# Three constant tables loaded in part and completed on the chip, mirrored x columns, a new order list (2-D spectral filter with a gate, one Trainium2 core)

## The chip, the cores and the metric

One core of a Trainium2 chip. Its engines are TensorE (PE; the loading of its stationary operand is shown apart as PEld), VectorE (DVE), ScalarE (ACT), GpSimd (POOL) and SyncE (SP), which here only issues DMAs. Each engine runs its own queue of instructions in order and waits at semaphores for the others. The metric is the device time of one execution in microseconds, the median of several runs.

## The reference

x has 2048 rows (S) and 1024 columns (D), in bf16. The sigmoid of each row's product with a gate vector gives g. x is taken through a real 2-D FFT, multiplied by two complex weight arrays (A and B), each product goes back through the inverse FFT, and the two results are mixed row by row:

```python
g = sigmoid((x * gate_w).sum(-1, keepdims=True))
X = rfft2(x)
a = irfft2(X * (A_w_r + 1j * A_w_i))
b = irfft2(X * (B_w_r + 1j * B_w_i))
return g * a + (1 - g) * b
```

## The kernel before

All transforms are matmuls with constant tables. A row index is s1 + 16 * s2, so the length-2048 transform is done in two factors, 128 and 16, with a twiddle between them; columns are split into four quarters of 256, folded by symmetry into an even half (par 0, units 0 to 7) and an odd half (par 1, units 8 to 15). The stages:

1. `F1` (f1, L336): for each s1 and each parity (e, o) 8 matmuls of 128x128 over s2, into PSUM. The fold y = a + b, a - b (L422) is done for 24 of the 32 pieces on DVE (`FC`, a copy of one half to SBUF by ACT, then `FD`, two additions on DVE) and for 8 on POOL, which can't read PSUM (`FX`, a copy of the whole by ACT or DVE, then `FP`, two additions on POOL). The copies go to eight slots of the tile wx.
2. For each of 16 units n: `F2` (L528, the column transform with the table FD, two tiles tt), `T` (its copy, by ACT or DVE: all copies stand on L201 for ACT, L203 for DVE), `F3` (L569, the twiddle and 16-point transform with the tables WF and WN; WN is the negated second half of WF, made by `neg`, L280), `X` (its copy), `P` (L586, the product with the weights W, one DVE instruction of 4096 elements), `J` (L632, the inverse 16-point transform with the table WJ) and two copies `R` into rl, which `H` (L654) stores to a scratch in DRAM. For units 0 to 7 the column 0 needs the partner row: `Y` (PE, table PM), `NA` (L609, DVE, with the pair weights WP) and `N` (L615, DVE), which patches the product before `J` reads it.
3. The gate: `gc` (L285 to L297, thirteen small instructions on POOL) makes its stationary operand gwz, `GH` (L447) multiplies it with y on PE, then `GC`, `Gt`, `GK`, `GZ`, `GS` (sigmoid on ACT), `GA` and `GB` (L515, L519, DVE) make the gate-weighted tables EA and EB from E.
4. `pw` (L313 to L320, eight small instructions on POOL) makes WP from w0.
5. `L` (L665) loads the scratch back, turned: eight loads of 512 KB for par 0 into re, eight for par 1 into ro. `V` (L675, with EA and EB), its copy `VC`, then the last transform with the table IG: `C` (i3f, L712) and `U` (i3, L703). For the even half `EX`, `EQ`, `E`, `ES`, `EF` (copies and the sum and difference, L796 and L806) write EV; for the odd half `OR` (L826, DVE), or `OC` and `OP` (ACT, then POOL, L822), or `QD` and `QP` (DVE, then POOL, L833 and L838) add and subtract, and `S` (L847) stores.

The order of everything is the list ORDER, written out by hand: each token is a call, for example `FD:3:e`, `P:1:b`, or `R:15:0:D`, whose last letter is the engine (A, D, P; S for the SP queue, on which all loads `x`, `c`, `W`, `L` and stores `H`, `S` stand). Each engine gets its instructions in the order of the list, whatever the others do. PSUM banks are the digits at the end of PE's tokens.

The tables WF, WJ and IG hold each value several times: WF is block-sparse (half of each block zero), WJ has six blocks of which three are others negated or exchanged, IG has its second half negated as a third block. All are loaded whole from DRAM. The lines that hold them:

```python
c["F1"] = _bf16np(np.concatenate([F, -F, F], axis=1))
G = np.concatenate([IG[:, 0], IG[:, 1], -IG[:, 1]], axis=-1)
c["IG"] = _bf16np(G.transpose(2, 0, 1, 3))
lh = C["WJ"][r, 2 * u + tt, w:w + 64]
```

Of the kernel before, what the change touches and what calls it, by code (L numbers as in the profile page):

```python
# [39 lines left out]
P:5:b NA:5:D N:5:D F3:6:6 J:4:2:0 F2:8:0:5 P:7:b X:6:A Y:6:4 NA:6:D R:4:0:A P:6:b R:4:1:A T:8:0:A J:5:2:6 F2:9:0:1 R:5:0:A  # L40
Y:7:0 F2:9:1:5 R:5:1:A F3:8:2 NA:7:D T:9:0:D F2:10:1:0 T:9:1:D F2:10:0:4 X:8:A T:10:1:A N:7:D GA:D:8 T:10:0:A F3:9:2 GA:D:4
W:S:14 H:2:1 X:9:A J:7:6:0 N:6:D GA:D:0 P:8:b J:6:2:4 W:S:12 H:2:0 R:7:1:A H:3:1 R:6:0:D W:S:15 R:7:0:A H:5:0 H:5:1 GB:D:4
P:9:b H:4:1 R:6:1:A F3:10:0 H:4:0 X:10:A H:7:1 F2:11:0:6 F2:11:1:7 F2:12:0:4 H:6:0 F2:12:1:5 F2:13:1:0 F2:14:1:1 P:10:b
T:11:0:A T:11:1:A T:12:0:A T:12:1:A F3:11:6 J:8:4:2 X:11:A F3:12:6 T:14:1:A R:8:0:A T:13:1:A F2:13:0:1 GB:D:0 R:8:1:D
# [867 lines left out]
```

## Time and profile before

| | us |
|---|---|
| median of 3 runs | 114.50 (114.27 to 114.72) |
| the profiled execution | 114.51 |
| its span, first to last instruction | 112.7 |
| DVE busy | 100.1 (89%) |
| PE busy | 99.4 (88%) |
| ACT busy | 86.2 (76%) |
| POOL busy | 43.0 (38%) |
| DMA: 36.79 MB | 326 GB/s over the span |

A row of the timeline gives the start, the length, the engine, the line, the operation, the output and input with their shapes, and how many instructions were merged; in brackets the idle time before it and what ended that. Instructions on one engine overlap a little at their ends, so the step from one start to the next is less than the length shown. In the chain of waits a row is the start, the time, and what the end of the kernel waited for.

### The profile page before, as it was taken

Reading aid. Unit: us, or ns where it says so; the run is one execution under the profiler, and the core shown is the slowest. Engines: PE = TensorE matmul, PEld = TensorE weight load, DVE = VectorE, ACT = ScalarE, POOL = GpSimd, SP = SyncE. Lnnn points to the kernel's source line nnn. Section 1 sums busy time; section 2 is a strip of 40 time slices with the busy share of each in tenths; the row PEclk is TensorE's granted clock in tenths of the full one; section 3 lists DMA queues with packets and bytes.
Section 4 is the critical chain, followed back from the end, with each engine's and each line's share of the span. In section 5 each row is a group of like instructions: output and inputs, shape, how many; then the busy total and the mean of one; then the engine's idle time right before and its main releaser. Section 6 shows DMA issues by size and latency. Waiting matters only on the chain.

```text
span 112.7 us, 3824 instructions
## 1 busy us (share of the span) xinstructions
PE 99.4 (88%) x1556; PEld 69.8 (62%) x1559; DVE 100.1 (89%) x160; ACT 86.2 (76%) x141; POOL 43.0 (38%) x64
## 2 busy tenths in 40 slices
...
DVE  0278999999999999999999999999999678999770
ACT  4176887899999999999999999998867934435300
POOL 3187969700000000000000007178702269999760
...
DMA  3999999989999999985799999999889998444994
GB/s 70 368 309 398 405 379 400 398 260 413 410 412 412 372 298 326 394 298 186 237 302 292 420 407 307 385 377 325 295 246 398 337 385 329 196 192 186 372 372 186
DMA packets 17794, 36.79 MB, mean 326 GB/s; under 512 B 1904, under 2 KB 10736, under 8 KB 17776
## 3 DMA queue, kind: packets, MB, share of 16 engines
...
q10 hardware_dynamic: 288, 0.10, 0.4%
...
## 4 chain that ended last, share of the span: by engine, by line
PE 32%; DVE 27%; DMA 16%; ACT 10%; issue 7%; SPq 4%; DVEq 1%; ACTq 0%
DVE p L586 9%; DVE y L422 9%; PE ps L703 8%; DMA ro<-sc 6%; DMA re<-in_x_dram 5%; DVE rl L203 5%; PE ps L632 5%; PE ps L528 5%; PE ps L675 5%; DMA sc<-rl 5%; ACT rl L201 4%; PE ps L569 4%; ACT T L201 3%; SPq L665 3%; PE ps L336 3%
## 5 line engine op out<-in xcount | busy, mean ns | idle before, releaser
L806 POOL TENSOR_TENSOR re<-wx 128x256 f32<-128x256 f32 x10 | 10.7, 1089 | 55.8 <-ACT wx L201 55.8
L201 ACT COPY wx<-ps 128x256 f32<-128x256 f32 (+1 forms) x41 | 18.3, 475 | 8.0 <-PE ps L336 4.5
L201 ACT CAST rl<-ps 128x1024 bf16<-128x1024 f32 x23 | 22.8, 1069 | 0.8 <-PE ps L632 0.6
L201 ACT CAST V<-ps 128x512 bf16<-128x512 f32 x26 | 14.9, 616 | 8.8 <-PE ps L675 4.4
L632 PE MATMUL ps<-p,wj 32*64 32x512 bf16 x512 | 18.2, 380 | 1.1 <-ACT rl L201 0.6
L528 PE MATMUL ps<-fd,y 128*128 128x256 bf16 x128 | 17.1, 273 | 1.3 <-ACT T L201 0.8
L586 DVE TENSOR_TENSOR p<-X,ro 128x4096 bf16<-128x4096 bf16 x8 | 18.2, 2278 | 0.0
L201 ACT CAST X<-ps 128x1024 bf16<-128x1024 f32 x16 | 17.3, 1079 | 0.1
L422 DVE TENSOR_TENSOR y<-ps,wx 128x256 bf16<-128x256 f32 x48 | 16.4, 414 | 0.5 <-ACT wx L201 0.5
L336 PE MATMUL ps<-f,re 128*128 128x128 bf16 x256 | 15.2, 219 | 1.6 <-DMA re<-in_x_dram 1.5
L336 PEld LDWEIGHTS <-re 128*128 128x128 bf16 x256 | 14.6, 98 | 2.4 <-DMA re<-in_x_dram 2.2
L201 ACT CAST T<-ps 128x512 bf16<-128x512 f32 x26 | 15.5, 647 | 0.5 <-PE ps L528 0.3
L528 PEld LDWEIGHTS <-y 128*128 128x128 bf16 x128 | 11.3, 97 | 5.9 <-issue 4.5
L632 PEld LDWEIGHTS <-wj 32*64 32x64 bf16 x512 | 8.3, 103 | 7.6 <-issue 4.1
L422 POOL TENSOR_TENSOR y<-wx 128x256 bf16<-128x256 f32 x16 | 11.3, 732 | 2.6 <-ACT wx L201 2.1
L826 DVE TENSOR_TENSOR ot<-re,ps 128x512 bf16<-128x512 f32 x18 | 11.3, 682 | 0.9 <-PE ps L703 0.4
L703 PE MATMUL ps<-ig,V 128*128 128x512 bf16 x45 | 11.2, 379 | 0.2
L712 PE MATMUL ps<-ig,V 128*128 128x256 bf16 x80 | 10.9, 273 | 0.2 <-ACT rl L201 0.2
L203 DVE CAST rl<-ps 128x1024 bf16<-128x1024 f32 x9 | 10.9, 1215 | 0.2 <-PE ps L632 0.2
L569 PE MATMUL ps<-T,wf 64*64 64x512 bf16 (+1 forms) x128 | 10.1, 333 | 1.1 <-DVE rl L203 0.4
L838 POOL TENSOR_TENSOR ot<-pq 128x512 bf16<-128x512 f32 x8 | 10.0, 1281 | 0.0
L675 PEld LDWEIGHTS <-re 128*128 128x128 bf16 x128 | 7.8, 98 | 2.4 <-issue 1.3
...
## 6 DMA issues: line engine op xcount, KB each, us to landing
...
```

Source lines behind the costliest of these rows:

```text
L201: nc.scalar.copy(out=out, in_=in_)
L203: Q[e].tensor_copy(out=out, in_=in_)
L336: nc.tensor.matmul(o, lhsT=lh, rhs=rh, start=(h == 0), stop=(h == 1))
L422: Q[e].tensor_tensor(yo[:, v, k:k + n, s1, :], a.rearrange("p (k c) -> p k c", c=4), b.rearrange("p (k c) -> p k c", c=4), op)
L528: nc.tensor.matmul(ps[:, v * 256:v * 256 + 256], lhsT=y[:, v, par, b, 2 * t:2 * t + 2, :, :].rearrange("p j s c -> p (j s c)"), rhs=C["FD" ...
L569: nc.tensor.matmul(view(ps[ho, tt * 512:(tt + 1) * 512], dst), lhsT=lh, rhs=view(T[hp(jh), tt, :], src), start=(w == 0), stop=(w == 1))
L586: nc.vector.tensor_tensor(p[:], xb, wb, ALU.mult)
L632: nc.tensor.matmul(o, lhsT=lh, rhs=src[r, ri, wi, tt], start=(q == 0), stop=(q == 3))
L675: nc.tensor.matmul(ps[:, ch * 128:ch * 128 + 128], lhsT=RR[par][:, v, ch // 2, s, c0 + 256 * ab:c0 + 256 * ab + 128], rhs=Ew[:, s1, :], st ...
L703: nc.tensor.matmul(ps, lhsT=Vs[par, v][:, s, ch, :], rhs=rh, start=(ch == 0), stop=(ch == 3))
L712: nc.tensor.matmul(ps[:, o:o + 256], lhsT=Vs[par, v][:, s, ch, :], rhs=g[:, o:o + 256], start=(ch % 2 == 0), stop=(ch % 2 == 1))
L826: nc.vector.tensor_tensor(otile(v)[:, s, h, :], EV[:, v, s], PS["O", 1, v, s], (ALU.add, ALU.subtract)[h])
```

## The change

- **Tables.** F1 keeps two of three blocks. WF is loaded with 32 instead of 64 columns a block into a part of the tile EA that is free until `GS`, and `kW` (spread_wf) writes both halves of each block by two scales with a mask per partition. WJ is loaded with its first 64 of 192 columns, and `kJ` makes the other two blocks: 0 negates the whole, 1 negates every second pair, 2 copies the other pairs. IG is loaded with 1024 of 3072 columns, and `kI` (spread_ig, six parts) makes the mirrored and negated blocks with a sign per partition. `mk` (signs) makes masks and signs from a column of F1.
- **Mirrored columns.** Each quarter of x has its second 128 columns in reverse, on the host's side and in the tables FD and IG, so that the second half of an IG block is the first times a sign.
- **Where.** On POOL: `kW:0:4:1`, `kJ:0:4` 0, 1 and 2, `kW:4:16` 0 and 1, `kJ:4:16:2`, and all six `kI`; on DVE: `mk`, `kW:0:4:0`, `kJ:4:16` 0 and 1. `gc` and `pw` come after `kJ:4:16:2` on POOL.
- **Order.** A new list. Between engines move: one `FX`, net two `R`, one `T`, three `VC`, `E` from DVE to ACT; two `X`, one each of `EX`, `OC`, `ES` from ACT to DVE; two `EQ` from DVE to POOL. Loads: W:3, PM and both parts of WJ earlier; FD:1:2, W:2, EZ and IG later or among others; W:13 earlier; `H:8` before the `L:0`, `L:0:3` with the other `L:0`; the sequence of `L:1` is 1, 3, 6, 0, 5, 7, 2, 4 instead of 1, 3, 6, 7, 0, 2, 4, 5.
- `prod_part`, the argument `at` of load_w and the changed i3_half are called by neither list.

```diff
 ORDER = """
-warm:8 c:A:F1 x:S:0:1 x:S:1:1 c:A:gws F1:0:o:4 x:S:2:2 F1:0:e:1 F1:1:e:6 F1:1:o:5 FC:0:e:A FC:1:e:A tab:A x:S:4:2 x:S:6:2
-c:S:E x:S:8:2 FX:0:o:D x:S:10:2 FD:0:e FD:1:e F1:2:e:7 F1:3:e:2 F1:3:o:0 FX:1:o:D FC:3:e:A F1:2:o:5 F1:5:e:4 x:S:12:2
-c:S:WF:0:4 x:S:14:2 c:S:w0 gc:P FP:0:o FX:3:o:A FP:1:o FC:2:e:D F1:4:e:6 FC:5:e:A FD:2:e FD:3:e c:S:FD:0:1 c:S:WJ:0:4
...
-FP:7:o FP:5:o pw:P F1:12:o:4 FC:14:e:A F1:8:o:1 F1:10:o:5 FC:12:o:A FC:8:o:A FD:14:e FC:10:o:A neg:D:0:4 neg:D:4:16 FD:13:o
-F2:1:1:2 F2:1:0:6 F2:0:0:3 FC:15:o:A T:1:1:A FD:10:o FD:8:o FD:12:o T:1:0:A W:S:2 W:S:6 T:0:0:A F1:14:o:7 F2:0:1:5 F1:11:o:6
-T:0:1:A F3:1:2 FD:15:o FC:11:o:A F2:2:0:5 F2:2:1:4 FC:14:o:A X:1:A F3:0:0 FD:11:o T:2:0:A T:2:1:A X:0:A F2:4:1:6 F2:3:1:5
-FD:14:o Y:1:4 T:3:1:A P:1:b F2:4:0:3 F2:3:0:2 Y:0:7 F3:2:0 GH:5 T:3:0:A T:4:0:A NA:1:D W:S:10 W:S:5 P:0:b W:S:3 W:S:7
-c:S:WJ:4:16 F3:3:3 X:2:A W:S:9 NA:0:D T:4:1:A W:S:11 N:1:D W:S:4 GC:A J:1:6:0 F2:5:0:2 F2:5:1:5 P:2:b X:3:A R:1:1:A R:1:0:A
...
-V:0:2:0:2 VC:0:2:1:A VC:0:2:0:A EX:1:1:A H:12:0 J:14:0:4 J:13:6:2 R:14:0:A P:15:b H:11:1 R:14:1:A R:13:0:A C:0:2:1:1
-C:0:2:0:5 EX:2:0:A H:12:1 EX:2:1:D V:0:1:0:4 GB:D:12 R:13:1:D J:15:0:6 V:0:6:1:5 VC:0:1:0:A C:0:1:0:2 R:15:1:A V:0:6:0:4
-H:14:0 H:14:1 GB:D:8 R:15:0:D H:13:0 H:13:1 VC:0:6:1:A H:15:1 H:15:0 VC:0:6:0:A V:0:4:1:3 V:0:5:1:6 L:0:3 EX:1:0:A L:1:1
-L:1:3 L:1:6 EQ:0:0:1:D C:0:6:1:0 V:0:5:0:4 VC:0:5:1:D VC:0:5:0:D E:6:1:A EQ:2:1:0:D EQ:0:1:1:P L:1:7 L:1:0 L:1:2 L:1:4
...
-OR:7:1:0 S:S:7:0 OR:7:1:1 S:S:6 OP:4:0:0 OP:4:0:1 OR:4:1:1 OR:4:1:0 S:S:7:1 S:S:4
+warm:8 c:A:F1 x:S:0:1 x:S:1:1 c:A:gws x:S:2:2 mk:D F1:0:o:1 F1:0:e:4 c:S:WF:0:4 x:S:4:2 x:S:6:2 x:S:8:2 c:S:PM c:S:WJ:0:4
+F1:1:o:5 x:S:10:2 c:S:E x:S:12:2 F1:1:e:0 x:S:14:2 tab:A FX:0:o:A W:S:3 c:S:w0 F1:2:o:7 FC:0:e:D FC:1:e:A F1:2:e:1 FP:0:o
+c:S:FD:0:1 c:S:WF:4:16 W:S:0 FD:0:e c:S:WJ:4:16 W:S:1 FX:1:o:A kW:0:4:1:P FD:1:e kW:0:4:0:D FX:2:o:D FC:2:e:A FP:1:o F1:3:e:4
+FP:2:o F1:3:o:0 FC:3:e:A neg:D:0:4 FD:2:e FD:3:e FX:3:o:A FP:3:o F1:5:e:3 F1:4:e:6 F1:5:o:5 FC:5:e:A FC:4:e:A FD:5:e FD:4:e
+F1:6:e:0 F1:7:e:1 kJ:0:4:1:P kJ:0:4:0:P F1:7:o:2 kJ:0:4:2:P F1:8:e:7 F1:9:e:4 FC:6:e:A FD:6:e F1:9:o:6 FC:7:e:A FX:7:o:A
...
+F1:14:e:1 F1:10:o:5 FC:15:e:A FC:12:o:A FC:14:e:A FP:4:o F1:13:o:3 F1:14:o:4 FC:10:o:A FD:13:e FC:13:o:A FC:14:o:A F1:8:o:6
+FD:15:e FC:8:o:A FD:14:e F2:1:0:1 F2:0:0:7 FD:10:o FD:13:o F1:15:o:0 kW:4:16:1:P FD:14:o T:1:0:A F2:1:1:5 F2:0:1:3 T:0:0:A
+F1:11:o:1 FD:8:o FC:15:o:A T:1:1:A T:0:1:A F3:1:6 c:S:FD:1:2 FD:12:o W:S:2 kW:4:16:0:P W:S:10 W:S:7 W:S:6 FD:15:o F3:0:3
+FC:11:o:A FD:11:o X:1:A X:0:A F2:2:0:2 W:S:4 W:S:5 W:S:9 W:S:11 F2:4:1:0 F2:2:1:5 F2:3:1:6 kJ:4:16:2:P gc:P Y:1:7 neg:D:4:16
+P:1:b pw:P T:2:1:A c:S:IG T:2:0:A F2:3:0:1 F2:4:0:4 F3:2:2 GH:5 T:3:1:A T:3:0:A X:2:A Y:0:6 T:4:0:A T:4:1:A F3:3:2 P:0:b
+NA:1:D NA:0:D N:1:D J:1:6:0 P:2:b F2:7:1:4 GC:A X:3:A R:1:0:A R:1:1:A Gt:2 Y:2:3 F2:5:0:5 T:5:0:A c:S:EZ N:0:D NA:2:D
+F2:5:1:3 H:1:0 W:S:8 H:1:1 T:5:1:A F3:4:6 P:3:b Y:3:5 T:7:1:A NA:3:D kJ:4:16:1:D F2:7:0:3 J:0:0:4 N:3:D X:4:A T:7:0:A kI:0:P
+kJ:4:16:0:D kI:3:P GK:D J:3:2:6 R:0:0:A kI:1:P R:0:1:D R:3:1:A Y:4:5 GZ:0:0 F2:6:1:4 F3:5:6 GS:0 N:2:D R:3:0:D H:0:0 NA:4:D
...
+H:10:1 EQ:1:0:1:P R:13:1:A H:10:0 H:12:1 GB:D:8 V:0:7:0:6 VC:0:7:0:A H:12:0 V:0:2:0:4 C:0:2:1:5 EQ:0:1:0:P VC:0:2:0:A
+EQ:1:1:0:P J:15:0:2 H:11:1 EX:2:1:A H:14:0 R:15:0:A R:15:1:D C:0:2:0:6 V:0:7:1:5 H:13:0 H:13:1 H:14:1 VC:0:7:1:A V:0:3:1:7
+V:0:5:0:4 C:0:7:0:2 C:0:7:1:1 EQ:1:1:1:D VC:0:5:0:A EX:7:0:A H:15:0 EQ:0:1:1:P H:15:1 V:0:5:1:0 V:0:3:0:4 V:0:4:0:2 EX:2:0:D
+EQ:2:1:1:D EQ:2:0:1:D VC:0:3:0:D VC:0:5:1:A kI:5:P EQ:1:0:0:P EQ:0:0:0:P EQ:7:0:1:P C:0:5:0:5 VC:0:3:1:A kI:4:P EQ:7:0:0:P
+EX:7:1:A L:1:1 L:1:3 C:0:5:1:3 L:1:6 L:1:0 VC:0:4:0:A C:0:3:1:4 V:0:6:1:7 C:0:3:0:0 V:0:4:1:1 V:0:6:0:6 L:1:5 L:1:7
+EQ:0:0:1:P EQ:7:1:1:P EQ:2:1:0:P EQ:7:1:0:P E:3:1:A ES:5:1:A ES:5:0:D EQ:2:0:0:D L:1:2 EF:5:0 C:0:4:0:2 EF:5:1 VC:0:6:1:A
...
     return 8 * t + 4 * (i % 2) + i // 2
+
+
+NF = 3 if "FG:" in ORDER else 2
+
+
+def quarter_order():
+    return np.concatenate([np.arange(128), 255 - np.arange(128)])
 def make_constants():
...
     F = F.reshape(128, 128)
-    c["F1"] = _bf16np(np.concatenate([F, -F, F], axis=1))
+    c["F1"] = _bf16np(np.concatenate([F, -F, F][:NF], axis=1))
     c["E"] = _bf16np(E)
...
     c["ID"] = _bf16np(np.eye(128))
-    j = np.arange(256) - 255.5
+    j = quarter_order() - 255.5
     i = np.arange(256)
...
     IG = IG.reshape(2, 2, 2, 128, 256)
-    G = np.concatenate([IG[:, 0], IG[:, 1], -IG[:, 1]], axis=-1)
-    c["IG"] = _bf16np(G.transpose(2, 0, 1, 3))
+    G = np.concatenate([IG[0, 0, :, :, :128], IG[0, 1, :, :, :128]], axis=-1)
+    c["IG"] = _bf16np(np.stack([G, IG[1, 0]]).transpose(2, 0, 1, 3).reshape(128, 1024))
     s1 = np.arange(NS1)
...
                     WJ[h, t, blk + 2 * cc] = v
-    c["WF"] = _bf16np(WF)
-    c["WJ"] = _bf16np(WJ.reshape(128, NT, 6, 2, 8, 2).transpose(0, 1, 2, 4, 3, 5).reshape(128, NT, -1))
+    keep = np.stack([WF[jj::2, :, :, 32 * jj:32 * jj + 32] for jj in range(2)], axis=1).reshape(128, NT, 2, 32)
+    c["WF"] = _bf16np(keep)
+    c["WJ"] = _bf16np(WJ.reshape(128, NT, 6, 2, 8, 2).transpose(0, 1, 2, 4, 3, 5).reshape(128, NT, -1)[:, :, 0:64])
     PM = np.zeros((2, 2, 128, 128))
...
     C = {}
-    for n, sh, dt in (("F1", [3, 128], BF16), ("FD", [2, 2, 2, 256], BF16), ("WF", [NT, 2, 64], BF16), ("WN", [NT, 64], BF16), ("PM", [2, 2, 128], BF16),
-                      ("IG", [2, 2, 768], BF16), ("E", [128], BF16), ("EZ", [128], BF16), ("ID", [128], BF16),
-                      ("WJ", [NT, 12 * NS1], BF16),
+    for n, sh, dt in (("F1", [NF, 128], BF16), ("FD", [2, 2, 2, 256], BF16), ("WF", [NT, 2, 64], BF16), ("WN", [NT, 64], BF16), ("PM", [2, 2, 128], BF16),
+                      ("IG", [2560], BF16), ("cf", [4], F32), ("E", [128], BF16), ("EZ", [128], BF16), ("ID", [128], BF16),
+                      ("WJ", [3, NT, 64], BF16),
                       ("EA", [NS1, 128], BF16), ("EB", [NS1, 128], BF16), ("zt", [NS1], BF16), ("one", [1], BF16), ("mk", [4], BF16),
...
     C["w0"] = C["EB"][:].rearrange("p a b -> p (a b)")[:, 1152:1408].rearrange("p (s u r t a w) -> p s u r t a w", s=2, u=NU, r=2, t=2, a=2)
+    wfk = C["EA"][:].rearrange("p a b -> p (a b)")[:, 1024:2048].rearrange("p (t w m) -> p t w m", t=NT, w=2)
     cnt = [0, 0]
...
         a, b = int(a), int(b)
-        if n in ("WF", "FD", "WJ"):
+        if n == "WF":
+            Q[q].dma_start(wfk[:, a:b], dr[n][:, a:b])
+        elif n == "WJ":
+            Q[q].dma_start(C[n][:, 0, a:b], dr[n][:, a:b])
+        elif n == "FD":
             Q[q].dma_start(C[n][:, a:b], dr[n][:, a:b])
+        elif n == "IG":
+            Q[q].dma_start(C[n][:, 0:1024], dr[n])
         elif n == "gws":
...
                 f"p {' '.join('abcd'[:len(dr[n].shape) - 1])} -> p ({' '.join('abcd'[:len(dr[n].shape) - 1])})"))
-    def load_w(q, n):
+    def load_w(q, n, at=""):
         n = int(n)
-        if n < 8:
+        if at:
+            w = Re[:, int(at) * 2048:(int(at) + 1) * 2048]
+        elif n < 8:
             w = Ro[:, n * 2048:(n + 1) * 2048]
...
         Q[q].dma_start(w, w_in[n // NU][n % NU])
+
+    def scale(e, out, in_, k):
+        if e == "A":
+            nc.scalar.mul(out, in_, k)
+        else:
+            Q[e].tensor_scalar(out, in_, k, None, ALU.mult)
+
+    def signs(e):
+        s = C["F1"][:, 0, 2:3]
+        for k, (m, a) in enumerate(((1.0, 0.0), (-1.0, 0.0), (0.5, 0.5), (-0.5, 0.5))):
+            Q[e].tensor_scalar(C["cf"][:, k:k + 1], s, m, a, ALU.mult, ALU.add)
+
+    def spread_wf(a, b, g, e):
+        a, b, g = int(a), int(b), int(g)
+        scale(e, C["WF"][:, a:b, :, 32 * g:32 * g + 32], wfk[:, a:b], C["cf"][:, 2 + g:3 + g])
+
+    def spread_wj(a, b, k, e):
+        a, b = int(a), int(b)
+        W = C["WJ"]
+        s, t = [W[:, i, a:b].rearrange("p t (g b s) -> p (t g) b s", b=2, s=2) for i in (0, 2)]
+        if k == "0":
+            scale(e, W[:, 1, a:b], W[:, 0, a:b], -1.0)
+        elif k == "1":
+            scale(e, t[:, :, 0], s[:, :, 1], -1.0)
+        else:
+            cp(e, t[:, :, 1], s[:, :, 0])
+
+    def spread_ig(k, e):
+        G = C["IG"]
+        ev, od = [G[:, o:o + 512].rearrange("p (b c m) -> p b c m", b=2, c=2) for o in (0, 512)]
+        er, os_, on = [G[:, o:o + 512].rearrange("p (b c m) -> p b c m", b=2, c=2) for o in (1024, 1536, 2048)]
+        pl, mi = C["cf"][:, 0:1], C["cf"][:, 1:2]
+        o, i, c = ((er[:, :, 0], ev[:, :, 0], pl), (er[:, :, 1], ev[:, :, 1], mi), (os_[:, :, 0], od[:, :, 1], pl), (os_[:, :, 1], od[:, :, 0], pl),
+                   (on[:, :, 0], od[:, :, 1], mi), (on[:, :, 1], od[:, :, 0], mi))[int(k)]
+        scale(e, o, i, c)
+
+    def ig(par, b, ch):
+        G = C["IG"]
+        if par == 0:
+            o = 256 * b + 128 * ch
+            return G[:, o:o + 2048].rearrange("p (h m) -> p h m", h=2)[:, :, 0:128]
+        o = 512 + 256 * b + 1024 * ch
+        return G[:, o:o + 256]
     def neg(e, a, b):
...
                         r = slice(64 * H + 32 * j, 64 * H + 32 * j + 32)
-                        lh = C["WJ"][r, 2 * u + tt, w:w + 64]
+                        lh = C["WJ"][r, w // 64, 2 * u + tt, :]
                         o = pss[tt][hp(H ^ tt), j * 512:(j + 1) * 512].rearrange("p (a m) -> p a m", a=2)
...
         for ch in range(4):
-            g = C["IG"][:, par, ch % 2]
-            rh = bc(g[:, 0:256]).to_broadcast([P, 2, 256]) if ch < 2 else g[:, 256:768]
+            if ch < 2:
+                rh = bc(ig(1, ch, 0)).to_broadcast([P, 2, 256])
+            else:
+                rh = C["IG"][:, 1536:2560].rearrange("p (g b m) -> p g b m", g=2, b=2)[:, :, ch - 2]
             nc.tensor.matmul(ps, lhsT=Vs[par, v][:, s, ch, :], rhs=rh, start=(ch == 0), stop=(ch == 3))
...
             o = (ch // 2) * 256
-            g = C["IG"][:, par, ch % 2]
-            nc.tensor.matmul(ps[:, o:o + 256], lhsT=Vs[par, v][:, s, ch, :], rhs=g[:, o:o + 256], start=(ch % 2 == 0), stop=(ch % 2 == 1))
+            nc.tensor.matmul(ps[:, o:o + 256], lhsT=Vs[par, v][:, s, ch, :], rhs=ig(par, ch % 2, ch // 2), start=(ch % 2 == 0), stop=(ch % 2 == 1))
...
 def quarters():
-    j = np.arange(256)
+    j = quarter_order()
     return np.concatenate([j, 511 - j, 512 + j, 1023 - j])
...
```

More of the change, by code (lines that the diff above doesn't have):

```diff
@@ L40 @@
[L40 to L44, printed above, removed]
@@ L65 @@
+S:S:2 S:S:6 OR:7:1:1 OR:7:1:0 OR:4:1:1 OC:4:0:A OR:4:1:0 S:S:7:0 OP:4:0:0 S:S:7:1 OP:4:0:1 S:S:4
 """
@@ L589, in prod, with prod_part @@
         nc.vector.tensor_tensor(p[:, int(r)], xb, w, ALU.mult)
+    def prod_part(n, r, t, e):
+        n, r, t = int(n), int(r), int(t)
+        if n not in Ps:
+            Ps[n] = wk.tile([P, 2, 2, 4, 256], BF16, name="p", tag="p", bufs=PB)
+        xb = Xs[n][:, r, t].rearrange("p (a m) -> p a m", a=1).to_broadcast([P, 4, 256])
+        Q[e].tensor_tensor(Ps[n][:, r, t], xb, Ws[n][:, t], ALU.mult)
     def parts(n, k):
```

52 lines of the change are left out of this document (25 added, 27 removed).

## The prediction

> **What bounds the kernel now.** I read the engines' shares and slices first, then the table of stretches, the waits, the timeline from 19 to 46 us, and last the chain that ended last.
>
> ```profile
> DVE  0278999999999999999999999999999678999770
> ACT  4176887899999999999999999998867934435300
> POOL 3187969700000000000000007178702269999760
> ...
> DMA  3999999989999999985799999999889998444994
> ```
>
> A slice is 2.8 us. DVE is full from slice 5 (about 11 us) to slice 30 (about 85 us); ACT joins it from 23 to 75 us. POOL stands idle from 22 to 66 us. DMA is nearly full until 48 us.
>
> ```profile
> 70.00:75.00 5.00, 4.84 (x100) 2.81 (x100) 5.00 (x4) 5.00 (x9) 1.74 (x2) 1.00 1.09 381
> ...
> 85.00:90.00 5.00, 4.95 (x67) 4.24 (x66) 4.23 (x12) 4.24 (x10) 1.46 (x2) 1.00 1.01 370
> ```
>
> Columns: stretch, length, busy us of PE, PEld, DVE, ACT and POOL, clock, DMA share, GB/s. Until 75 us DVE and ACT are the limit; from 85 us PE is, at 4.95 of 5, and DVE, ACT and POOL have gaps.
>
> ```profile
> PE ps L675 <- DMA ro<-sc: 0.5, 1, 0.5
> ```
>
> Among the waits no product (L586) waits for a load. The DMA waits that cost PE are those for x before 7.8 us (1.5) and two in the tail: this one at about 87 us, and one of 0.46 that the timeline shows before 92.92.
>
> ```profile
> 24.89 2.27 DVE L586 TENSOR_TENSOR p<-X,ro 128x4096 bf16<-128x4096 bf16 x1
> 27.09 0.18 DVE L609 TENSOR_TENSOR np<-ps,wp 128x32 f32<-128x32 f32 x1
> 27.19 2.27 DVE L586 TENSOR_TENSOR p<-X,ro 128x4096 bf16<-128x4096 bf16 x1
> ...
> 68.38 2.43 POOL L806 TENSOR_TENSOR re<-wx 128x256 f32<-128x256 f32 x1 [46.57 <-ACT wx L201]
> ...
> 76.31 0.72 POOL L806 TENSOR_TENSOR re<-wx 128x256 f32<-128x256 f32 x1
> 76.37 0.94 DVE L519 TENSOR_TENSOR eb<-e,ea 128x512 bf16<-128x512 bf16 x1
> ```
>
> From start to start a product takes 2.20 us, `NA` 0.10. The rows at 68.38 and 76.31 decide the forecast: a POOL addition of 0.73 us (median) that meets the product of 67.94 to 70.22 takes 2.43 and ends at 70.81, 0.6 after it; the DVE `GB` that meets a POOL addition takes 0.94 instead of 0.60. So products and POOL operations on SBUF run one after the other.
>
> ```profile
> 79.00 1.15 DVE rl L203
> 80.15 0.02 issue
> 80.16 2.38 DMA sc<-rl
> ...
> 85.72 7.16 DMA ro<-sc
> ...
> 104.06 3.47 PE ps L703 x16
> ```
>
> The chain: DVE's last `R`, its store, the exchange loads, then PE to 107.53, and after it only DVE's last rows and the store.
>
> **The change, part by part.** The sum goes against the profiled execution, 114.51 us (span 112.7, 1.8 around it); the median of the three runs is 114.50.
>
> *Loads.* F1 96 to 64 KB, WF 512 to 256, WJ 768 to 256, IG 768 to 256: 1,312 KB less, 3.4 us of DMA time at the 400 GB/s of the busy slices. No product waits for a load, and the shorter backlog brings none forward that is waited for: I take 0. Bounds 0 and -3.4.
>
> *First stage, to the first product.* DVE loses one `FX` (0.61 start to start) and gains `mk` (in its idle time, before 4.9), `kW:0:4:0` and nothing else; a 256-element scale (L280) took 0.575 us beside a POOL addition and a 768-element one 0.425 when that had ended. It starts on `FC:0:e` 0.5 later, because `F1:0:e` is second on PE. x for s1 = 2 lands at 7.7 as before, WF:0:4 right behind it (64 KB, 0.2), so `kW:0:4:0` at about 8.1, `FX:2` 8.5, `neg:0:4` (waits for `kW:0:4:1` on POOL, 8.6) 9.1, `FD:2` 9.6. Then 22 `FD` of 0.70 and `neg:4:16` of 0.34: the first product at 25.3 against 24.89, +0.4. Bounds: -0.6 (the work alone) and +1.2 (each of three scales waits a POOL addition, 0.7, less what overlaps). PE's 32 `F1` of 0.47 stay ahead; later x pieces come 0.3 late behind PM and WJ, and PE is then behind them. The table load, at 6.2 before, moves into ACT's idle time.
>
> *POOL up to the first `NA`.* This is the term that decides. Before, `gc` was done at 6.1 and `pw` at 21.8. Now they stand behind the eight `FP` (1.41 each), five scales and two copies. No row shows POOL scaling bf16 by a pointer. Lower bound: its memset of 256 elements, 0.308 us, which over the 0.094 of one element is 0.84 ns per element; upper: its additions, 0.732 at 256 and 1.272 at 512, 2.1 ns per element. One input lies between none and two, so I take the middle: 256 elements 0.55, 768 elements 1.3 (bounds 0.75 and 1.8), 384 0.7, 128 0.35. Walk: `FP:0` 5.95 to 7.35; `kW:0:4:1`, after WF lands, to 8.6; three `FP` to 12.8; `kJ:0:4` 1, 0, 2 to 14.05; four `FP` to 19.7; two `kW:4:16` to 22.3; `kJ:4:16:2` to 23.0; `gc` (2.0 as before) to 25.0; `pw` needs 1.95 more. The products run 25.3 to 29.8. One of `pw`'s eight gets in before, one between the two products; six remain, 1.5 us, and `NA:1` waits for them on DVE: with `NA:0`, `N:1` and product 2 behind it, and `J:1` on PE. By the stretches DVE is idle for 0.3 us in all from 25 to 80, so the end moves by 1.5 plus the 0.2 of the one between: +1.7. Bounds: 0 (lower prices, by which the same walk ends at 24.8) and +3.1 (`pw` whole and the five reading operations of `gc`, 1.1).
> The Trainium skill, GPSIMD Engine Reference, section Engine selection, puts one-input elementwise work on GpSimd at roughly line rate. By that the scales lie at the lower bound and the sum is that of the first rival below, 114.5; no row of this case shows such an operation.
>
> *Middle, product 1 to the last `R`.* DVE: two `R` (1.14) and one `T` (0.60) go, two `X` (1.14) and two `kJ:4:16` (0.34 and 0.43, by the 768-element row) come: +0.2. ACT: two `R` and one `T` and one `VC` more, two `X` less (0.91, 0.48, 0.49, 0.88): +1.0, which lies beside DVE's wait; without that wait up to +1.0 would show. `kI:0, 3, 1, 2`, 0.55 each, fall on POOL among products: each can hold one back as at 76.31. Four times between 0 and 0.55 (0 to 1.2 with the two later ones in DVE's idle time): +0.4. `kJ` must precede `J:3`; it does, by `R:0:0`'s place.
>
> *SP queue.* W:3 comes early, FD:1:2 and W:2 late. W:10 waits for the last `FD` as before (4.0 us of SP), now with W:7, 6, 4, 5 behind it: from 22.6, at 1.3 us each, they land by about 31, and product 4 starts after 37. `H:8` now goes ahead of the exchange loads `L:0`, all eight of which precede `H:9`: rl buffers free earlier. IG and EZ land by about 35, `GZ` comes after 36. 0. If IG were later, `kI` would move with it, and only `C` at 66 reads it.
>
> *Layouts.* Matmuls and their columns are the same in number; a moving operand read in two blocks is no new thing (L703 reads half of its operands as a broadcast, minimum and median 379 ns). Mirrored x columns change no transfer's size. 0.
>
> *Tail.* After `J:15` PE has 9 `V` instead of 10 of par 0 left (0.45). `L:0:3` no longer stands between `H:15` and `L:1` (512 KB, 1.3 us), and `L:1:0` is fourth, not fifth: the two PE waits (0.5 and 0.46) should go. POOL's 14 closing operations from 91.04 to 109.0 follow `U:1:1:0`, which comes 0.9 earlier after `J:15`, but two `EQ` and two `kI` (2.6 us) more lie ahead of them, in the 8.4 us that POOL idles from 81 to 91. What DVE and ACT swap (`E`, `EQ`, `VC`, `ES`, `EX`, `OC`) lies in their gaps there (DVE 3.90 of 5, ACT 1.83 of 5 from 90 to 95); were PE not the bound, ACT's `VC` would cost 0.5 each. -1.0; bounds -1.4 and 0.
>
> Sum: 0.4 + 1.7 + 0.2 + 0.4 - 1.0 = +1.7: 116.2 us, with its own range from 114.8 to 117.5.
>
> **The rivals.**
> *POOL is done in time* (0.24). The prices lie at the lower bound and `NA:1` waits for nothing; 0.4 + 0.2 + 0.4 - 1.0 = 0.0: 114.5. For it: it needs only that one-input operations run like the memset. Against it: it leaves 0.5 us, my walk lets POOL idle nowhere after 7.4, and before it idled 2.6 us among the `FP`.
> *The loads were the limit* (0.12, faster). The 1,312 KB go from the path: at slices 2 to 17 every later load starts earlier, and the exchange with them: 114.5 - 3.4 = 111.1. It decides if products turn out to have waited for W, by some 0.5 us each. Against it: no such wait is in the list, and DVE is full there.
> The Trainium skill, SBUF — State Buffer, section A bandwidth-pool intuition that's wrong, says that HBM is almost always the end-to-end bottleneck, which would make this the outcome; the trace does not agree, with DVE full from 11 to 85 us at 326 GB/s mean.
> *`gc` is caught too* (0.14). If POOL reaches `gc` 1 us later, its reads wait for both products, `GH` blocks PE until about 31, and `NA:1` waits 3.1: 0.4 + 3.1 + 0.2 + 0.4 - 1.0: 117.6.
>
> **How the numbers follow.** Forecast 0.50, rivals 0.24, 0.12, 0.14. A measurement tells about 0.5% (0.57 us) from no change. Faster: 0.12 + 0.10 of the second case (tail at its best) + 0.06 of the forecast = 0.28. Same: 0.08 + 0.04 = 0.12. Slower: 0.40 + 0.06 + 0.14 = 0.60. The range 113.0 to 118.2 leaves out the load case and the top of the last.
>
> **What would show it.** Right: the first L609 row about 2 us after the second product ends, with an idle gap put down to POOL; `pw` rows stretched above 0.26 us; POOL's scales near 1.3 us; PE's waits at 87 and 92 us gone; DMA slices below 9 before 48 us. Wrong: `pw` ending before the first product starts; POOL scales below 0.8 us; the first `NA` right behind the second product; or, for the load case, `J:15` some 3 us earlier than 76.85 with DVE less full than before.

## The result and the profile after

| | before | after |
|---|---|---|
| median, us | 114.59 (114.27 to 115.35, 6 runs) | 119.35 (119.16 to 119.79, 6 runs) |
| the profiled execution, us | 114.51 | 119.22 |
| its span, us | 112.7 | 117.4 |
| POOL busy, us | 43.0 | 60.0 |
| DMA, MB | 36.79 | 35.45 |

The ratio after to before is 1.040 [1.036, 1.045]: slower by 4.7 us between the two profiled executions (4.8 between the medians), where 1.7 us had been forecast, and above the range given, which ended at 118.2. Disturbed executions are left out of the ratios here and below but not of the medians, so the two need not agree to the last digit.

The slices of the page of after (one is 2.94 us):

```profile
DVE  0169999999159899999999999999989758999870
ACT  4157869999049999999999999999988575544400
POOL 1089999999907910000000000008799439999770
PEclk9999999999769999999999999999999999999997
DMA  3999999899942869999385799999964999519594
```

DVE and ACT have a hole in slices 10 and 11 (counted from 0), at 29 to 35 us, that they did not have before. POOL, which had been idle from 22 us, is now full until 32. The granted clock of PE, at 9 everywhere else but in the last slice, is 7 and 6 in the same two slices, and DMA has little to move in slices 11 and 12 (4 and 2 tenths).

The table of stretches of after (columns as before: stretch, length, busy us of PE, PEld, DVE, ACT, POOL, clock, DMA share, GB/s); the last two answer to those at 70 and 85 us before:

```profile
25.00:30.00 5.00, 2.33 (x31) 1.61 (x28) 4.71 (x3) 4.52 (x8) 4.58 (x9) 1.00 1.02 410
30.00:35.00 5.00, 4.73 (x74) 2.03 (x82) 1.42 (x4) 1.03 (x2) 2.14 (x10) 0.66 0.71 275
75.00:80.00 5.00, 4.74 (x100) 3.14 (x99) 5.00 (x5) 5.00 (x9) 0.32 (x1) 1.00 1.04 356
90.00:95.00 5.00, 4.68 (x54) 3.60 (x52) 3.21 (x9) 3.14 (x7) 2.26 (x4) 1.00 0.99 388
```

In the first, PE is busy for 2.33 of 5 us. In the second, DVE works for 1.4 of 5 us; PE's 4.73 go into 74 matmuls at a clock of 0.66. The later stretches are limited as before: DVE and ACT at 5.00 of 5, then PE.

The waits of after (waiter, line, who was waited for: us, times, longest):

```profile
PE ps L508 <- POOL gwz L357: 2.9, 1, 2.9
DVE np L677 <- POOL wp L381: 2.5, 1, 2.5
DVE np L677 <- PE ps L669: 1.4, 1, 1.4
...
PE ps L743 <- DMA ro<-sc: 0.2, 1, 0.2
```

L508 is `GH`, which waits for gwz, what `gc` makes; L677 is `NA`, first for `pw`'s last row, then for `Y`, which stands behind `GH` on PE. The wait of the tail, 0.5 us before, is 0.2.

DVE and POOL in the timeline of after, from the first product (L647) to the third:

```profile
25.24 4.47 DVE L647 TENSOR_TENSOR p<-X,ro 128x4096 bf16<-128x4096 bf16 x2
32.17 0.19 DVE L677 TENSOR_TENSOR np<-ps,wp 128x32 f32<-128x32 f32 x1 [2.46 <-POOL wp L381]
33.77 0.19 DVE L677 TENSOR_TENSOR np<-ps,wp 128x32 f32<-128x32 f32 x1 [1.41 <-PE ps L669]
33.88 0.22 DVE L683 TENSOR_TENSOR p<-np 128x16 bf16<-128x16 f32 x1
33.96 2.28 DVE L647 TENSOR_TENSOR p<-X,ro 128x4096 bf16<-128x4096 bf16 x1
```

```profile
19.96 4.40 POOL L297 TENSOR_SCALAR wf<-ea,cf 128x768 bf16<-128x768 bf16 x2
24.30 0.52 POOL L212 COPY wj<-wj 128x384 bf16<-128x384 bf16 x1
...
25.84 1.78 POOL L353 TENSOR_SCALAR gh<-gws 128x8 f32<-128x8 bf16 x1
27.69 2.08 POOL L354 TENSOR_TENSOR gh<-gh 128x4 f32<-128x4 f32 x1
29.73 0.20 POOL L355 TENSOR_TENSOR gh<-gh 128x4 f32<-128x4 f32 x1
...
30.15 0.21 POOL L358 TENSOR_TENSOR gwz<-gh 128x4 bf16<-128x4 f32 x1
...
31.79 0.35 POOL L381 TENSOR_SCALAR wp<-wp 128x32 f32<-128x32 f32 x1
```

The third product before, and the first of those `gc` operations before:

```profile
29.57 2.28 DVE L586 TENSOR_TENSOR p<-X,ro 128x4096 bf16<-128x4096 bf16 x1
```

```profile
4.99 0.24 POOL L292 TENSOR_SCALAR gh<-gws 128x8 f32<-128x8 bf16 x1 [3.33 <-DMA gws<-in_gw_dram]
```

The two scales kW:4:16 take 2.2 us each, not 1.3. So `gc` begins at 24.74, and its two operations at 25.84 and 27.69, which take 0.24 and 0.20 us where no product runs (they are next to nothing: 8 and 4 elements), get in one per product. `gc` ends at 30.36, `pw` at 32.14. In between lies PE, whose rows show what `GH` then cost:

```profile
30.27 3.14 PE L508 MATMUL ps<-y,gwz 128*32 128x512 bf16 x32 [2.94 <-POOL gwz L357]
```

Before, the same 32 matmuls took 1.91 us:

```profile
27.41 1.91 PE L447 MATMUL ps<-y,gwz 128*32 128x512 bf16 x32
```

The chain that ended last runs through exactly these rows:

```profile
14.47 5.53 POOL y L483 x8
19.99 4.37 POOL wf L297 x2
...
25.84 1.79 POOL gh L353
...
27.69 2.08 POOL gh L354
...
30.27 3.14 PE ps L508 x32
```

POOL has 17% of the chain; before it had none.

Where the 4.7 us lie, from the two profiled executions (start of the row named; the end is that of the execution's time):

| | before | after | difference |
|---|---|---|---|
| first product | 24.89 | 25.24 | +0.35 |
| first to third product | 4.68 | 8.72 | +4.04 |
| third product to the last row of `J` | 47.28 | 48.12 | +0.84 |
| last row of `J` to the last row of `U` | 27.05 | 26.53 | -0.52 |
| last row of `U` to the end | 10.61 | 10.61 | 0 |

### The profile page after: what moved, and what is told of

The parts are those of the page before. It is cut to its first block, busy times and chain, and to the rows that moved or that the text cites. A ratio compares the mean times of both kernels' runs of the same rounds, so it can differ in the third digit from the quotient of the medians.

```text
span 117.4 us, 3848 instructions
## 1 busy us (share of the span) xinstructions
PE 102.3 (87%) x1559; PEld 71.5 (61%) x1559; DVE 99.4 (85%) x162; ACT 87.2 (74%) x143; POOL 60.0 (51%) x79
## 2 busy tenths in 40 slices
DMA packets 17795, 35.45 MB, mean 302 GB/s; under 512 B 1905, under 2 KB 10993, under 8 KB 17777
## 4 chain that ended last, share of the span: by engine, by line
PE 37%; POOL 17%; DMA 16%; ACT 13%; DVE 7%; issue 5%; SPq 1%; DVEq 1%; ACTq 0%
PE ps L773 8%; PE ps L700 8%; POOL y L483 7%; DMA sc<-rl 7%; ACT rl L210 6%; DMA re<-sc 5%; PE ps L743 5%; DMA ro<-sc 4%; POOL wf L297 4%; PE ps L255 3%; PE ps L781 3%; PE ps L508 3%; PE ps L397 2%; ACT T L210 2%; PE ps L589 2%
## 5 line engine op out<-in xcount | busy, mean ns | idle before, releaser
L874 POOL TENSOR_TENSOR re<-wx 128x256 f32<-128x256 f32 x12 | 9.7, 829 | 39.2 <-ACT wx L210 38.3
L210 ACT CAST rl<-ps 128x1024 bf16<-128x1024 f32 x25 | 25.4, 1087 | 0.7 <-PE ps L700 0.5
L210 ACT COPY wx<-ps 128x256 f32<-128x256 f32 (+1 forms) x39 | 17.4, 476 | 8.3 <-PE ps L397 5.8
L210 ACT CAST V<-ps 128x512 bf16<-128x512 f32 x29 | 16.9, 631 | 8.0 <-PE ps L743 4.3
L647 DVE TENSOR_TENSOR p<-X,ro 128x4096 bf16<-128x4096 bf16 x8 | 18.1, 2287 | 0.0
L397 PE MATMUL ps<-f,re 128*128 128x128 bf16 x256 | 16.1, 228 | 0.7 <-DVE y L483 0.7
L397 PEld LDWEIGHTS <-re 128*128 128x128 bf16 x256 | 15.8, 103 | 1.5 <-issue 1.0
L210 ACT CAST X<-ps 128x1024 bf16<-128x1024 f32 x14 | 14.7, 1072 | 0.7 <-PE ps L630 0.5
L773 PE MATMUL ps<-ig,V 128*128 128x512 bf16 x48 | 11.8, 379 | 0.1
L890 POOL TENSOR_TENSOR ot<-re,wx 128x512 bf16<-128x512 f32 x6 | 7.6, 1278 | 4.2 <-DVE wx L212 3.6
L297 POOL TENSOR_SCALAR ig<-ig,cf 128x256 bf16<-128x256 bf16 x6 | 7.5, 1256 | 3.9 <-DMA ig<-cst_ig 3.9
```

What stands on the lines that cost most here:

```text
L210: nc.scalar.copy(out=out, in_=in_)
L297: Q[e].tensor_scalar(out, in_, k, None, ALU.mult)
L397: nc.tensor.matmul(o, lhsT=lh, rhs=rh, start=(h == 0), stop=(h == 1))
L647: nc.vector.tensor_tensor(p[:], xb, wb, ALU.mult)
L773: nc.tensor.matmul(ps, lhsT=Vs[par, v][:, s, ch, :], rhs=rh, start=(ch == 0), stop=(ch == 3))
```

## The experiments

Theory: `gc` and `pw` come late because the work ahead of them on POOL is dearer than taken; their reads then meet the products; that stall is the 4.0 us. Rivals: only `pw` matters; the new list or the loads cost the time. In the diffs, tokens that don't matter are left out.

**1. `gc` ahead of the `FP`, as before the change.**

```diff
-... F1:2:e:1 FP:0:o ... kJ:4:16:2:P gc:P Y:1:7
+... F1:2:e:1 gc:P FP:0:o ... kJ:4:16:2:P Y:1:7
```

> Changed kernel with one edit: the gate's thirteen small POOL instructions (gc) stand ahead of the first FP, where POOL is idle, instead of behind kJ:4:16:2. Theory (POOL's small reading instructions are shut out by the two products, and GH on PE waits for gc): pw starts at about 24.8, two of its eight get in before the first product at 25.2, one between the products, five after them; the first L609-type row (NA) follows the second product by 1.1 us instead of 2.5, GH no longer blocks PE, the third product starts at about 31.0 instead of 33.96, and the time is about 116.4 (3.0 less than 119.35). Rival (the loss lies elsewhere in the new list, in the order of loads or the share between engines, and the wait only hides it): the third product comes earlier but the time stays above 118.3.

116.75 us, ratio 1.020 [1.012, 1.028]. Its timeline, POOL and then DVE:

```profile
24.92 0.41 POOL L374 TENSOR_TENSOR wp<-eb 128x32 f32<-128x32 bf16 x1
25.28 2.30 POOL L375 TENSOR_TENSOR wp<-eb 128x32 f32<-128x32 bf16 x1
27.54 2.30 POOL L377 TENSOR_TENSOR wp<-eb 128x32 f32<-128x32 bf16 x1
29.80 0.25 POOL L378 TENSOR_TENSOR wp<-eb 128x32 f32<-128x32 bf16 x1
```

```profile
31.03 0.29 DVE L677 TENSOR_TENSOR np<-ps,wp 128x32 f32<-128x32 f32 x2 [1.31 <-POOL wp L381]
```

Now it is `pw` that gets one operation in per product, and `NA` waits 1.31 us. `GH` takes 1.91 again, and the second wait is gone: the third product starts at 31.35, 2.6 earlier. This is the case that the prediction took for the likeliest, and from the first to the third product it costs 1.54 us (6.22 against 4.68), where the sum had 1.7. PE then had 2.05 us without work ahead of the first `J`, and in the profiled execution its clock fell here too, to 0.79 from 30 to 35 us and 0.87 in the next 5. That execution (117.81) is the slowest of the four; the mean clock of the others was higher (0.987 to 0.996 against 0.98).

**2. `pw` ahead of `gc`.**

```diff
-... kJ:4:16:2:P gc:P Y:1:7 neg:D:4:16 P:1:b pw:P
+... kJ:4:16:2:P pw:P gc:P Y:1:7 neg:D:4:16 P:1:b
```

> Changed kernel with one edit: pw stands ahead of gc on POOL, both still behind kJ:4:16:2. Theory (gc is the costlier of the two, since GH blocks PE and with it Y:0 and NA:0): NA:1 comes at about 30.9, but gc ends at about 32, GH at 34, so NA:0 and the third product start at about 34 as before: 118.9 to 119.8. Rival (only pw matters, because NA:1 waits for it, and gc is harmless): the third product starts at about 31 and the time is near 116.5.

122.54 us, ratio 1.070 [1.063, 1.076]. The first wait of `NA` shrinks to 1.30 and the second grows (DVE and PE in the timeline):

```profile
36.73 0.19 DVE L677 TENSOR_TENSOR np<-ps,wp 128x32 f32<-128x32 f32 x1 [5.65 <-PE ps L669]
```

```profile
32.76 3.60 PE L508 MATMUL ps<-y,gwz 128*32 128x512 bf16 x32 [5.44 <-POOL gwz L357]
```

The time is above the expectation too (119.8 at most). So not only `pw` matters: behind `gc` stands `GH`, behind it `Y`, and behind that `NA:0`. After 5.4 us without work, `GH` takes 3.60.

**3. Nothing of `gc` and `pw` near the products, kW:4:16 on ACT.** `gc` as in 1, `pw` behind the last `FP`, and

```diff
+... FC:12:o:A kW:4:16:1:A FC:14:e:A ... FD:13:e kW:4:16:0:A FC:13:o:A
```

> Changed kernel with gc ahead of the first FP, pw right behind the last FP, and the two large scales kW:4:16 on ACT among its copies of the first stage instead of POOL. Theory: no POOL instruction that anything waits for is left beside the two products; the third product starts at 29.6 to 30.0, and the time is 115.0 to 115.6, about 0.5 to 1.0 above the kernel before, which is what the middle (0.9 us) and the first stage (0.3) lose and the tail (0.6) gains. Rival (the new list itself loses): 117 or more. A load-bound kernel would come out below 112.5 here.

116.51 us, ratio 1.017 [1.011, 1.023], later than expected. `NA` waits for nothing, but the first product starts only at 26.47: on ACT, 0.94 us each, the scales stand ahead of copies that DVE waits for, and the first waits another 1.2 us for its load. The stall is gone and another place pays. ACT in the timeline:

```profile
19.63 0.94 ACT L295 ACTIVATE wf<-ea,cf 128x768 bf16<-128x768 bf16 x1 [1.18 <-DMA ea<-cst_wf]
```

**4. The same with kW:4:16 on DVE,** right ahead of neg:4:16.

```diff
+... kJ:4:16:2:P Y:1:7 kW:4:16:1:D kW:4:16:0:D neg:D:4:16 P:1:b
```

> Changed kernel, all tables completed on the chip, with gc ahead of the first FP, pw right behind the last FP and the two large kW:4:16 on DVE in front of neg:4:16 instead of POOL. Theory: they cost DVE about 0.7 to 0.9 us (a 768-element scale takes 0.42 there), the first product starts at about 25.9, no NA waits, the third product starts at about 30.3, time 115.3 to 115.9, the best that the completion on the chip gets here. Rival (some other wait takes the place): 117 or more.

115.16 us, ratio 1.004 [1.000, 1.008], the profiled execution 114.38. Run again:

> The kernel with `gc` early, `pw` behind the last FP and kW:4:16 on DVE once more, on the same chip as the one without kI. Theory: 115.0 to 115.4 us, third product at about 29.7. Rival (the first measurement was low by chance): 115.6 us or more.

115.46 us, ratio 1.006 [1.003, 1.009]. DVE in the timeline of the first:

```profile
23.92 0.74 DVE L297 TENSOR_SCALAR wf<-ea,cf 128x768 bf16<-128x768 bf16 x2
24.69 0.36 DVE L341 TENSOR_SCALAR wn<-wf 128x768 bf16<-128x768 bf16 x1
24.97 4.49 DVE L647 TENSOR_TENSOR p<-X,ro 128x4096 bf16<-128x4096 bf16 x2
29.37 0.28 DVE L677 TENSOR_TENSOR np<-ps,wp 128x32 f32<-128x32 f32 x2
```

The pair that costs POOL 4.40 us costs DVE 0.74. All three tables are still completed on the chip and the loads still cut; four moved tokens take back some 4 of the 4.7 us.

**5. Before's list with 1,280 KB less loaded.** Of WF, WJ and IG only the first block is loaded and used for all (the tables are not completed, so this leaves part of the computation out).

```diff
-    c["WF"] = _bf16np(WF)
+    c["WF"] = _bf16np(WF[:, :, 0])
...
-                        lh = C["WJ"][r, 2 * u + tt, w:w + 64]
+                        lh = C["WJ"][r, 2 * u + tt, 0:64]
```

> Kernel before, with its own list, but WF, WJ and IG loaded only with 256, 256 and 256 KB (1,280 KB less) and never completed: the matmuls read the loaded part again, same shapes, so the output is not the reference's. Theory (no load of this stage is waited for): 114.2 to 114.8, no change. Rival (the loads are the limit): 111.1 to 112.5, with J:15 some 2 to 3 us earlier than 76.85.

114.72 against 114.71 us, ratio 1.000 [0.996, 1.004]; third product at 29.43. In before's list the loads are worth nothing that the runs can tell.

**6. The new list with whole tables,** no kW, kJ, kI, mk.

> Changed kernel with its own list and mirrored columns, but WF, WJ and IG loaded whole (some 1.4 MB more) and mk, kW, kJ and kI gone. Theory (all of the loss before the third product is POOL's completion work pushing gc and pw into the products; loads are not waited for): gc and pw end by about 22.5, the first product starts near 24.6, the third at 29.0 to 29.6, J:15 and the end follow, without kJ and kI in the middle, some 84.4 to 85.0 later: 113.4 to 114.6, at or below the kernel before. Rival (the new list itself, or the load order, is the loss): 115.5 or more.

115.92 us, ratio 1.011 [1.005, 1.017]: the rival's case, not the theory's. (1.18 MB more were loaded than in after, not 1.4.) There is no stall at `NA`, but PE's timeline shows why the first product starts at 26.07:

```profile
15.87 4.34 PE L408 MATMUL ps<-f,re 128*128 128x128 bf16 x73 [1.69 <-DMA re<-in_x_dram]
```

The new list loads WF:0:4, PM and WJ:0:4 among the pieces of x; whole they are 192 KB more, and x is late by 2.1 us in all. In this list the loads do matter, at one place.

**7. Only WF whole.**

```diff
-            Q[q].dma_start(wfk[:, a:b], dr[n][:, a:b])
+            Q[q].dma_start(C[n][:, a:b], dr[n][:, a:b])
```

> Changed kernel with only WF loaded whole (256 KB more) and its four kW gone; kJ, kI, mk and the list stay. Theory: POOL is free of 4 scales (5.3 us), gc and pw end before the first product, the third product starts at 29.0 to 29.6, and with kJ on DVE and kI on POOL in the middle the time is that plus 85.3: 114.3 to 115.0. The difference to the kernel with whole tables is then the price of kJ and kI, 0.5 to 1.0. Rival (kJ and kI cost as much as kW): 116 or more.

115.84 us, ratio 1.011 [1.004, 1.018], later than expected. POOL is free early, at 19.7, but its next instruction is a copy that waits for WJ:

```profile
21.57 0.50 POOL L212 COPY wj<-wj 128x384 bf16<-128x384 bf16 x1 [1.91 <-DMA wj<-cst_wj]
```

WJ is no later here than in the first kernel of experiment 11, which loads WF in part and whose copy, after a wait for WJ too, starts at 21.87. In after POOL came to this copy only at 24.3, so that no wait showed. `gc` and `pw` wait behind it and `pw` is caught once more (`NA` waits 1.30).

**8. Is the clock part of it?** The changed kernel with 13 matmuls of 512 columns ahead of `GH`, into a buffer that nobody reads.

```diff
-... F3:2:2 GH:5 T:3:1:A
+... F3:2:2 warm:13:5 GH:5 T:3:1:A
```

> Changed kernel with thirteen idle matmuls of 512 columns on PE between F3:2 and GH, where PE otherwise waits 2.9 us for gwz (about 2.8 us of them); they write the bank that GH overwrites, and nothing reads them. Theory (GH took 3.14 us instead of 1.91 because the granted clock fell to 0.66 in that stage after the idle time, and NA:0 waited for what follows GH): GH takes about 1.9, NA:0 comes at 32.4 instead of 33.77, the third product at about 32.5, and the time is about 117.9. Rival (GH is slow for another reason, or the wait for pw alone sets the third product): no change, 119 or more.

119.74 us, ratio 1.041 [1.032, 1.050], with x late by 1.70 us at one place of the profiled execution. Run again:

> The changed kernel with 13 more matmuls of 512 columns on PE ahead of `GH`, writing to a buffer that nobody reads, so that PE is not idle while `gc` is being made. Theory (PE's idle time before `GH` lowers the granted clock, and with it `GH` and what follows take longer, about 1.2 us of the 4.0): `GH` 1.9 us, the second product not held by PE, third product about 32.7, time 117.9 to 118.5 us. Rival (the clock costs nothing on the path, DVE being held by `pw` anyway): 119 us or more.

119.54 us, ratio 1.036 [1.030, 1.042]; the profiled execution 119.12, span 117.3. PE and DVE in its timeline:

```profile
30.15 1.91 PE L508 MATMUL ps<-y,gwz 128*32 128x512 bf16 x32 [0.64 <-POOL gwz L357]
```

```profile
32.05 0.19 DVE L677 TENSOR_TENSOR np<-ps,wp 128x32 f32<-128x32 f32 x1 [2.46 <-POOL wp L381]
32.41 0.19 DVE L677 TENSOR_TENSOR np<-ps,wp 128x32 f32<-128x32 f32 x1 [0.16 <-PE ps L669]
```

```profile
30.00:35.00 5.00, 4.85 (x97) 2.63 (x98) 2.78 (x7) 2.67 (x4) 2.15 (x11) 1.00 0.62 240
```

The clock is 1.00 from 30 to 35 us, `GH` is back at 1.91, and from the first to the third product it is 7.48 us in place of 8.72. So 1.2 of the 4.0 us of the stall are PE's lower clock. The last row of `J` comes 1.5 us earlier too, but the end does not; among PE's waits from 80 us on:

```profile
PE ps L743 <- DMA ro<-sc: 1.7, 2, 1.5
```

After had 0.2 there. In this execution the tail, which waits for the exchange's loads, took 27.95 us (26.53 after) and gave the gain back: in the chains of waits the load that PE waits for was issued 1.4 us earlier (87.1 against 88.5) but took 5.8 us instead of 4.5. By their times both runs are the rival's case, 119 us or more. A gain in time is not shown.

**9. Whole tables behind x.** As 6, with `gc` early and WF:0:4, PM, WJ:0:4 loaded behind x (W:3 and neg:0:4 come later too).

```diff
-... F1:0:e:4 c:S:WF:0:4 x:S:4:2 x:S:6:2 x:S:8:2 c:S:PM c:S:WJ:0:4 ... x:S:14:2
+... F1:0:e:4 x:S:4:2 x:S:6:2 x:S:8:2 ... x:S:14:2 c:S:WF:0:4 ... c:S:WF:4:16 c:S:PM c:S:WJ:0:4
```

> The new order list with whole tables (no copies, no multiplications), `gc` ahead of the first FP, and the whole WF:0:4, PM and WJ:0:4 behind the last x load instead of among them; W:3 one place later, neg:0:4 later. Theory (the loss is the work given to POOL; the list and the loads are not at fault once the whole tables keep out of x's way): first product about 24.3 us, third about 28.9 with no wait of `NA`, time 113.4 to 114.4 us. Rival (the new list itself costs time behind the third product, or the 1,280 KB do): third product at 29 or later and 115.0 us or more.

115.61 us, ratio 1.003 [0.999, 1.006], later than expected. The first product comes as the theory has it, at 24.42, the third at 29.46 instead of 28.9, and the profiled execution (117.09, 1.5 us above the median of this kernel, so the wait need not be as long in the others) has a later wait on PE:

```profile
39.16 0.62 PE L553 MATMUL ps<-ez,zt 128*128 128x128 bf16 x8 [2.20 <-DMA ez<-cst_ez]
```

EZ (32 KB) is needed at 36.7 before, and its load was issued at 13.0. The new list issues it behind the loads W and IG: here, with whole tables ahead of it, at 29.1, and it lands 10.0 us later. In the changed kernel it is issued at 26.0, lands at 36.1 and is first used at 41.6; in experiment 4, without the stall, it lands at 35.2 and is used at 37.1. Of all the runs it is late here only.

**10. The same with EZ loaded ahead of FD:1:2,** about where it was before the change.

```diff
-... c:S:FD:1:2 FD:12:o ... T:5:0:A c:S:EZ N:0:D
+... c:S:EZ c:S:FD:1:2 FD:12:o ... T:5:0:A N:0:D
```

> The kernel with the new list and whole tables behind x, but EZ (32 KB) loaded ahead of FD:1:2, about where the kernel before loads it, in place of behind W:0 to W:11 and IG. Theory (the late EZ takes back what the first stage gains: PE waited 2.2 us for it): no wait for EZ, third product unchanged at about 29, time 113.3 to 114.4 us, faster than before. Rival (the new list is slower elsewhere, EZ's wait only stands in for the next one): 115.0 us or more.

114.36 us (before, measured beside it, 114.83), ratio 0.996 [0.993, 1.000], where experiment 9 had 1.003 [0.999, 1.006]: with whole tables EZ's place was worth some 0.6%. Its DVE rows:

```profile
24.14 4.50 DVE L658 TENSOR_TENSOR p<-X,ro 128x4096 bf16<-128x4096 bf16 x2
...
29.19 2.29 DVE L658 TENSOR_TENSOR p<-X,ro 128x4096 bf16<-128x4096 bf16 x1
```

This is the fastest version found, 0.4% below before, which its interval only just tells from no change: the new list, with none of the table work that it was paired with.

**11. kI.** Experiment 4's kernel with IG whole and no kI.

```diff
-            Q[q].dma_start(C[n][:, 0:1024], dr[n])
+            Q[q].dma_start(C[n][:], dr[n])
```

> As the kernel with `gc` early and kW:4:16 on DVE, but IG is loaded whole (+384 KB, late) and the six kI scales on POOL go. Theory (POOL's scales hold DVE's operations up among the products, the middle was 0.9 us longer than before's): third product unchanged at 29.7, J:15 0.3 to 0.6 us earlier behind it, time 0.2 to 0.5 us below that kernel's. Rival (the scales lie beside other work): the same time within 0.2 us, or more for the 384 KB.

115.04 us, ratio 1.003 [1.000, 1.006], against 1.006 [1.003, 1.009] for experiment 4 on the same chip: not told apart. From the third product to the last row of `J` it is 47.84 us with kI (47.83 in the second run) and 47.84 without. The theory falls: kI lies beside other work. And with EZ early as well:

> The kernel with gc early, kW:4:16 on DVE and IG whole, with EZ loaded ahead of FD:1:2 as well. Its trace showed no wait for EZ, its third product being 1 us later. Theory: no change, 114.8 to 115.3 us. Rival (EZ's lateness costs here too, in the executions that were not profiled): 114.5 us or less.

114.80 us, ratio 1.002 [1.000, 1.005]: no difference that can be told, as expected, since EZ was in time there.

## Why the prediction was wrong, step by step

*Right: that POOL decides, and how.* The walk had kW:4:16 begin at 19.7; it began at 19.96. It had `gc` and `pw` late, one small operation let in per product, `NA` waiting, and DVE without slack to make it up. All of that is in the rows.

*Wrong: the price in "POOL up to the first `NA`".* This is the step that failed: its term was +1.7, and from the first to the third product it measured +4.04. No row showed POOL scaling bf16 by a pointer; I took 1.3 us for 768 elements, between a memset (0.75) and its additions (1.8). It is 2.2, above my upper bound, and 0.93 at 256 elements (0.55 taken): by these two rows 2.5 ns an element and 0.3 us, dearer than an addition of two f32 inputs (2.1 ns, by 0.732 at 256 and 1.272 at 512). I argued that one input must cost less than two, and nothing in the profile said so. The copies came below the price I took: 0.52 at 384, 0.29 at 128 elements, or 0.87 ns an element.
The Trainium skill, GPSIMD Engine Reference, section Engine selection, has one-input work on GpSimd at roughly line rate. Here that holds of the copy, whose 0.87 ns an element is about the memset's 0.84, not of the multiplication, which costs nearly three times as much per element.

*So the case on record as a rival came, and larger.* `gc` began 1.7 us later than the walk had it, which is past the 1 us at which the rival "`gc` is caught too" decides. That rival said that `GH` blocks PE until about 31 and `NA:1` waits 3.1 us, 117.6 in all. In fact `GH` ended at 33.4. Two things were missing in it. By an end at 31 and its 1.91 us, `GH` would start at about 29.1; but three of the five reading operations of `gc` come behind the second product, which ends at 29.7, so `GH` starts at 30.27. And PE had by then nothing to do for 2.94 us, and got a clock of 0.66 from 30 to 35 us: `GH` 3.14 us instead of 1.91. Hence the second wait, 1.41 us, of `NA:0` for `Y`. The stall is 4.04 us: 1.5 of it remains if `gc` is early (6.22 us from the first to the third product in experiment 1, against 4.68), 1.2 goes with the clock (experiment 8), and the other 1.3 are the difference between experiments 8 and 1. Of these, 1.0 is that `pw` stands behind `gc` on POOL: the first `NA` comes 6.93 us after the first product in experiment 8 and 5.90 in experiment 1. The rest is the second `NA`, 0.16 of it its wait for `Y`. One sign fits this: `pw`'s rows, which the forecast had stretched, are 0.26 us in after, and `gc`'s are the stretched ones.
The Trainium skill, TensorE: Matmul & The Clock Gate, Part 1, lets PE's clock fall back after an idle window of about 3.4 us. Here 2.94 us without a matmul, in a stretch in which PE was busy for 2.33 of 5 us, was enough; in the profiled execution of experiment 1 the clock fell after 2.05 us.

*Loads, 0: right.* Experiment 5 is the test, with before's list: 1,280 KB less, ratio 1.000. The bandwidth rule cited in the prediction from the Trainium skill, SBUF — State Buffer, does not hold for this kernel's total. But the step left out where a load stands. Experiments 6 and 9 show two places in the new list (among x, and EZ) at which a load is waited for as soon as it is 192 KB longer or is issued 3 us later.

*SP queue, 0: right, by a small margin.* "IG and EZ land by about 35, `GZ` comes after 36": EZ landed at 36.1 and was used at 41.6. Without the stall it is still in time, by 1.9 us (experiment 4). With more loads ahead of it, it is not (experiment 9). I should have named that margin of 1 us, and what it costs when it is gone.

*First stage, +0.4: right* (the first product at 25.24 against 25.3).

*Middle, +0.6: 0.84, but not by its parts.* The 0.4 for kI among the products is not there: without kI the stretch is as long (experiment 11). With whole tables, thus without kJ and kI, it is still 47.90 us against 47.28 (experiment 10), and 47.81 to 47.84 in experiments 3, 4, 6 and 7. So some 0.5 to 0.6 belongs to the new list itself, and which of its moves does it was not tried.

*Tail, -1.0: -0.5.* The forecast counted one wait twice: the 0.5 in its list of waits and the 0.46 in its timeline are the same row, at 92.92, and the list has no other wait of PE from 78 us on. That wait became 0.2, at 93.47; the rest of the tail stayed with PE. Even this half is not clear of the scatter: the same stretch took 26.24 and 26.96 us in the two runs of experiment 4 and 27.22 in experiment 10, all with the new list, against 27.05 before.

*The rivals.* Nearest to "POOL is done in time" is experiment 4, with the two large scales on DVE: 115.2 to 115.5 against the 114.5 worked out. "The loads were the limit" fell with experiment 5.
